# Pooled q, k and v of the first batch made by TensorE from the local blocks' tiles

## Chip, cores, metric

The kernel runs on one core of a Trainium2 chip. The metric is the time of one execution in device microseconds (us), the median of several runs. Engines: PE is TensorE's matmuls, PEld its weight loads, DVE VectorE, ACT ScalarE, POOL GpSimd, SP SyncE, which issues most DMAs; a q behind the name (SPq) is the engine's instruction queue.

## What is computed

An attention block feeds two mixtures of dense layers, all in float32. B, H, S, D = 4, 8, 576, 64.

```python
def _attn_ref(q, k, v):
    Sd = S // 4
    q_d = q.reshape(B, H, Sd, 4, D).mean(axis=3)   # k_d, v_d likewise
    ...
    out_d = sm_attn(q_d, k_d, v_d)                  # attention over 144 pooled tokens
    out_up = np.repeat(out_d, 4, axis=2)
    pos = np.arange(S)
    mask = np.abs(pos[:, None] - pos[None, :]) < 4  # local: 3 tokens to each side
    scores = scale * np.matmul(q, k.transpose(0, 1, 3, 2))
    scores = np.where(mask, scores, -1000000000.0)
    ...                                             # softmax
    out_local = np.matmul(attn, v)
    return out_up + out_local
...
x = attn_out.transpose(0, 2, 1, 3).reshape(2304, 512)
h = x @ w_in;  x = (h * np.cos(h)) @ w_out          # d_ff 2048
xn = x / rms * rms_g                                # second mixture, d_ff 1536
out = (silu(xn @ w_gate) * (xn @ w_val)) @ w_out2
```

## The kernel before

The program is written by generators, one for each piece of work. A planner (class Order) runs them against assumed costs and emits every engine's instructions in the order of its own clock, preferring early due times among what is ready; on the chip each engine then executes its list in order. Buffers and PSUM banks are tokens in pools (take, give); events tie generators together (wait, done). Where the planner sees TensorE idle in the first stretch, keep_warm (L251) emits filler matmuls of ident.

**First batch, pooled branch.** start() loads q and k of batch 0 in groups of four tokens, three column groups each (tile pq, L861). pq_first sums four tokens (sum4: q by one VectorE reduction, L385; k by two GpSimd additions, L380 and L382), transposes the sums on TensorE (trq, L425) and pq_ev copies them to PQ (pqs, L401). v comes in four head pairs of four loads each (values0, pv_load, L480 and L483; tile v4); pv sums them on GpSimd (L504 to L511) into vh, a block-diagonal tile. pooled() makes the scores (sps, L539), the softmax (L544 to L560), transposes the weights (tra, L575), multiplies by v (avp, L594) and copies the result to od (L602).

**Local blocks.** Each batch has five blocks of 116 queries (112 in the last) with 128 keys around them. block() takes one block's q and k (tile raw, loaded by raw_dma, L798, a token in each partition, 256 bytes to a descriptor), transposes them (btr, L646), multiplies them in 64x64 pieces (bs, L690), takes the softmax (L699 to L712), transposes the weights (bat, L726), waits for od, multiplies by v (bav, L752; v lies in one of three buffers vb, loaded by block_v, L814), adds od (L762) and rounds the sum into a high and a low part of x (L775 on ScalarE, L777 on GpSimd).

**First mixture.** Token tile 0 (256 tokens) needs the blocks 0, 1 and 2 of batch 0, tile 1 the blocks 2, 3 and 4. unit() computes h = x @ w_in for two chunks (h, L1013), second() the product with w_out (y, L1079). The weights are loaded as int32 words (L291, L293) and converted by w_conv on ScalarE, VectorE and GpSimd (L316 to L327). Two units of tile 0 come first, then tiles 0 and 1 take turns.

**Order of the loads.** SP issues them in program order: pq of batch 0, the mask bf, and then by a written list, where "w" is weight pieces, "r" a block's raw tiles, "v" all of v4:

```python
LOADS = (("w", 4), ("r", 1), ("v", 0), ("r", 1), ("w", 4), ("r", 3))
```

The early tiles lie in places that weights use later; 21 of the 31 places are held at first.

Of the kernel before, what the change touches and what calls it, by code (L numbers as in the profile page):

```python
# [9 lines left out]
F32 = mybir.dt.float32  # L10
# [3 lines left out]
ALU = mybir.AluOpType  # L14
# [23 lines left out]
LOADS = (("w", 4), ("r", 1), ("v", 0), ("r", 1), ("w", 4), ("r", 3))  # L38
# [17 lines left out]
class Order:  # L56
# [136 lines left out]
def fused_kernel(ctx: ExitStack, tc, q, k, v, w_in, w_out, w_gate, w_val, w_out2, rms_g, mask, bmask, out):  # L193
# [86 lines left out]
    def w_loads(m, pieces, src):  # L280

        for i in pieces:
            S_.due(conv_due(m, i) - 5.0)
            r = yield take("raw")
            p = yield take(PLACES, 1)
# [90 lines left out]
    def sum4(b, w, t, o, n):  # L376

        if b or w:
            yield "POOL", 0.05 + n * 0.32
            POOL.tensor_tensor(out=t[:, :n, 0:2], in0=t[:, :n, 0:2], in1=t[:, :n, 2:4], op=ALU.add)  # L380
            yield "POOL", 0.05 + n * 0.18
            POOL.tensor_tensor(out=o, in0=t[:, :n, 0], in1=t[:, :n, 1], op=ALU.add)  # L382
        else:
            yield "DVE", 0.05 + n * 0.27
            DVE.tensor_reduce(out=o, in_=t[:, :n].rearrange("p u r d -> p u d r"), axis=AX.X, op=ALU.add)  # L385
# [28 lines left out]
    def pq_first(w, c, t, qs, place):  # L414

        u0, n = UC[c]
        yield wait(("pq", w, c))
        yield from sum4(0, w, t, qs[:, u0:u0 + n], n)
        give("pqp", place)
        yield take("att")  # L420
        i = yield take("bank")
        ps = bank_tile(i, [64, 4, 128], "trq")
        yield "PE", 0.2 * n
        for x in range(n):
            PE.transpose(ps[:, x, :], qs[:, u0 + x, :], ident)  # L425
        yield from pq_ev(0, w, c, ps)
        give("bank", i)
        give("att", "att")
        count(("pq", 0), 6)
# [57 lines left out]
    def pv(b, hp, t=None, place=None, vh=None):  # L487

        vi = 0
        if b == 0:  # L490
            yield wait(("pv", hp))
        else:
            vi = yield take("vh")
            vh = VH[vi]
            p = []
            for _ in range(2):
                x = yield take("pq")
                p.append(x)
            t = (ap.tile([128, 512], F32, tag=p[0], name="v4").rearrange("p (c x) -> p c x", c=2),
                 ap.tile([128, 512], F32, tag=p[1], name="v4")[:, :256])  # L500
            yield from pv_load(b, hp, *t)
# [10 lines left out]
        if b == 0:  # L512
            give(place[2], place)
        else:
            for x in p:
                give("pq", x)
# [3 lines left out]
    def pooled(b, hp, E=None):  # L520
# [72 lines left out]
        for c in range(3):  # L593
            PE.matmul(o, vh[:, c], A[:, c], start=c == 0, stop=c == 2)  # L594
# [35 lines left out]
    def block(b, u, raw, pools):  # L630
# [9 lines left out]
        for w in range(2):  # L640
# [4 lines left out]
            for a in range(4):  # L645
                PE.transpose(t[:, a, :], raw[w][:, 2 * a:2 * a + 2].rearrange("t h d -> t (h d)"), ident)  # L646
# [107 lines left out]
        give("vb", v_i)  # L754
# [46 lines left out]

    def block_v():

        for b in range(B):
            for u in range(5):
                S_.due(blk_due(b, u) - 5.0)
                x = yield take("vb")
                VI[b, u] = x
                r0 = geo(u)[2]
                vp = v[b].rearrange("(a e) t d -> e t a d", e=2)  # L810
                for s, (_, _, kc) in enumerate(groups(u)):
                    for e in range(2):
                        yield "SP", 0.5
                        SP.dma_start(VB[x][64 * e:64 * e + 64, s], vp[e, r0 + kc:r0 + kc + 64])  # L814
                done(("rv", b, u))
# [26 lines left out]
    def start():  # L842
# [3 lines left out]
        for n in [("pq", w, c) for c in range(3) for w in range(2)] + [("qs", w) for w in range(2)] + [("E", hp) for hp in (1, 2, 3)] \  # L846
                + [("v4", hp) for hp in range(4)] + [("vhl", 0)] + [("raw", u) for u in range(5)]:
            pl[n] = yield take(PLACES)
# [4 lines left out]
        def load(ev, us):  # L853
            yield "SP", us

        qs = [early(("qs", w), [128, 9, 64]) for w in range(2)]
        for c, (u0, n) in enumerate(UC):
            for w in range(2):
                t = early(("pq", w, c), [128, 4, 4, 64])
                yield "SP", max(0.48, 0.37 * n)  # L860
                SP.dma_start(t[:, :n], pq_src(0, w, u0, n))  # L861
                done(("pq", w, c))
                S_.add(pq_first(w, c, t, qs[w], pl["pq", w, c]), 0.0, S_.now())
# [5 lines left out]
        for hp in range(4):  # L869
            S_.add(pooled(0, hp, E[hp]), 0.0)  # L870
        vh0 = early(("vhl", 0), [128, 2, 3, 128])
        vh0 = VH + [vh0[:, 0], vh0[:, 1]]
        for x in vh0:
            yield "POOL", 0.5
            POOL.memset(x, 0.0)
# [13 lines left out]
        def values0():  # L889
            for hp in range(4):  # L890
                t = early(("v4", hp), [128, 768])
                t = t[:, :512].rearrange("p (c x) -> p c x", c=2), t[:, 512:]
                yield from pv_load(0, hp, *t)
                done(("pv", hp))
                S_.add(pv(0, hp, t, pl["v4", hp], vh0[hp]), 0.0, S_.now())
# [7 lines left out]
        def raws(us):  # L903
            for u in us:
                t = early(("raw", u), [128, 2, 8, 64])
                for w in range(2):
                    yield from raw_dma(t[:, w], (q, k)[w], 0, u)
                done(("raw", 0, u))
                S_.add(block(0, u, (t[:, 0], t[:, 1]), (None, (pl["raw", u][2], pl["raw", u]))), blk_due(0, u))

        first = 0
        for what, n in LOADS:
            if what == "r":
                yield from raws(range(first, first + n))
                first += n
            elif what == "w":
                yield from words(n)
            else:
                yield from values0()
# [6 lines left out]
        S_.add(after("vhl", None, pl["vhl", 0]), 0.0)  # L926
        S_.add(after(("pq", 0), None, pl["qs", 0], pl["qs", 1]), 0.0)
# [5 lines left out]
        yield wait(("E2", 2))  # L933
        for _ in range(3):
            p = yield take("pqp")
            give(p[2], p)
# [911 lines left out]
```

## Time and profile before

| what | us |
|---|---|
| median of 3 runs (lowest to highest) | 983.76 (983.52 to 984.35) |
| profiled execution | 984.96 |
| its span in the profile | 983.1 |
| PE busy | 953.0 (97%) |
| PEld busy | 880.4 (90%) |
| DVE busy | 721.2 (73%) |
| ACT busy | 542.3 (55%) |
| POOL busy | 269.1 (27%) |

The span is the time from the first to the last recorded instruction; start times count from its beginning. Busy shares are means over stages with different limits. Ends of matmuls are modelled, so the length of a group of them is rough, while starts are not. A releaser behind an instruction is what ended the idle time before it.

### The profile page before, as it was taken

The numbers are of one execution on the slowest core, as the hardware profiler recorded it, in microseconds if no ns is written. First come the engines' busy times: TensorE is split into PE (matmuls) and PEld (weight loads), VectorE is DVE, ScalarE is ACT, GpSimd is POOL, SyncE is SP. The second block draws the span as 40 slices with busy tenths as digits, with TensorE's granted clock in tenths as the row PEclk, the third lists the DMA queues.
The fourth block names the chain that finished last, engine by engine and source line by source line (L and its number), as shares of the span: only waits on it lengthen the run. The fifth ranks groups of instructions, "written<-read, shape, count | busy, mean of one in ns | idle before, by whom it ended". The sixth has DMA issues, their size and how long they took to land.

```text
span 983.1 us, 19205 instructions
## 1 busy us (share of the span) xinstructions
PE 953.0 (97%) x7150; PEld 880.4 (90%) x7150; DVE 721.2 (73%) x1460; ACT 542.3 (55%) x1090; POOL 269.1 (27%) x325
## 2 busy tenths in 40 slices
PE   6789899999999999999999999999999999999998
PEld 6688778888988888888888889999999999999998
DVE  2789976677657775666577699586666688999895
ACT  3658886677677965656566465242322334554442
POOL 3877685544336311101042242000000014300000
PEclk9999999999999999999999999999999999999999
DMA  8788643567685554544331311133222144454432
GB/s 241 212 211 246 181 147 111 148 199 180 199 231 166 170 171 128 176 144 169 120 129 65 107 44 49 49 106 93 75 82 71 57 145 132 132 174 139 141 119 76
DMA packets 160333, 136.07 MB, mean 138 GB/s; under 512 B 72176, under 2 KB 133744, under 8 KB 160240
## 3 DMA queue, kind: packets, MB, share of 16 engines
q1 hardware_dynamic: 160240, 134.85, 45.8%
q8 instruction: 56, 0.92, 0.4%
q14 instruction: 37, 0.30, 0.1%
HBM read 98.64 MB, written 36.18 MB: 137 GB/s over the span
## 4 chain that ended last, share of the span: by engine, by line
PE 84%; DMA 4%; DVE 3%; SPq 3%; issue 2%; POOL 2%; ACT 2%; DVEq 0%; POOLq 0%; ACTq 0%
PE gvp L1502 26%; PE y L1079 19%; PE h L1013 18%; PE o L1755 13%; PE bav L752 2%; PE btr L646 1%; DMA pq<-in_q 1%; DMA raw<-in_k 1%; PE avp L594 1%; PE bs L690 1%; PE yt L1407 1%; POOL wwa L327 1%; PE bat L726 1%; PE sps L539 1%; DMA cst<-in_moe_rms_g 1%
## 5 line engine op out<-in xcount | busy, mean ns | idle before, releaser
L1502 PE MATMUL gvp<-xc,wc 128*128 128x384 f32 x1296 | 231.7, 335 | 0.0
L1502 PEld LDWEIGHTS gvp<-xc,wc 128*128 128x128 f32 x1296 | 225.6, 188 | 0.3
L1573 DVE TENSOR_TENSOR tmp<-gvp,tmp 128x384 f32<-128x384 f32 x180 | 99.3, 553 | 54.3 <-PE gvp L1502 51.0
L1013 PE MATMUL h<-big,wwa 128*128 128x256 f32 (+1 forms) x756 | 124.0, 316 | 0.9 <-DVE t L1038 0.5
L1755 PE MATMUL o<-wo,wc 128*128 128x256 f32 x972 | 118.4, 279 | 0.0
L1013 PEld LDWEIGHTS h<-big,wwa 128*128 128x128 f32 x756 | 107.5, 190 | 10.7 <-DVE t L1038 0.6
L1755 PEld LDWEIGHTS o<-wo,wc 128*128 128x128 f32 x972 | 115.7, 190 | 0.0
L1079 PE MATMUL y<-wwa,big 128*128 128x512 f32 x432 | 109.5, 397 | 0.7 <-DVE big L1049 0.7
L1079 PEld LDWEIGHTS y<-wwa,big 128*128 128x128 f32 x432 | 78.9, 188 | 17.7 <-DVE big L1049 1.6
L1013 PE MATMUL h<-big,wwb 128*128 128x256 f32 (+1 forms) x504 | 83.9, 317 | 0.4 <-DVE t L1038 0.3
L1079 PE MATMUL y<-wwb,big 128*128 128x512 f32 x324 | 82.0, 398 | 1.1 <-POOL big L1049 1.1
L1033 DVE SCALAR_TENSOR_TENSOR t<-kk,h 128x512 f32<-128x512 int32 x72 | 49.0, 681 | 44.1 <-ACT kk L1031 43.9
L1013 PEld LDWEIGHTS h<-big,wwb 128*128 128x128 f32 x504 | 72.0, 190 | 7.8 <-DVE t L1038 0.8
L1031 ACT ACTIVATE kk<-h 128x512 int32<-128x512 f32 x72 | 42.6, 592 | 58.1 <-PE h L1013 55.8
L1079 PEld LDWEIGHTS y<-wwb,big 128*128 128x128 f32 x324 | 59.0, 188 | 13.3 <-POOL big L1049 1.4
L1639 POOL TENSOR_TENSOR wt<-wo 128x256 f32<-128x256 f32 x10 | 9.8, 985 | 208.6 <-DVE wc L1358 183.4
L1038 DVE TENSOR_TENSOR t<-h,t 128x512 f32<-128x512 f32 x72 | 49.3, 686 | 17.9 <-ACT t L1036 17.4
L1564 ACT ACTIVATE tmp<-gvp 128x384 f32<-128x384 f32 x36 | 17.7, 492 | 75.8 <-PE gvp L1502 75.8
L1036 ACT ACTIVATE t<-t,cst 128x512 f32<-128x512 f32 x72 | 51.9, 722 | 13.4 <-DVE t L1033 12.9
L1047 ACT ACTIVATE big<-t 128x512 fp32r<-128x512 f32 x72 | 45.1, 628 | 25.1 <-DVE t L1038 23.7
L1698 ACT ACTIVATE wc<-ut 128x512 fp32r<-128x512 f32 (+1 forms) x60 | 34.3, 584 | 42.2 <-DVE ut L1684 25.3
L1049 DVE TENSOR_TENSOR big<-t,big 128x512 fp32r<-128x512 f32 x54 | 39.8, 738 | 16.6 <-ACT big L1047 16.3
(189 smaller groups left out, 1741.2 us busy)
## 6 DMA issues: line engine op xcount, KB each, us to landing
us<-tmp SPq DMA_DIRECT2D x72, 192.0 KB, 2.0
uf<-us SPq DMA_DIRECT2D x48, 256.0 KB, 3.0
rawwa<-in_moe_w_out SPq DMA_DIRECT2D x21, 512.0 KB, 4.3
wfs<-rawwa SPq DMA_DIRECT2D x36, 256.0 KB, 2.4
rawwa<-in_moe_w_gate SPq DMA_DIRECT2D x12, 512.0 KB, 4.3
rawwa<-in_moe_w_val SPq DMA_DIRECT2D x12, 512.0 KB, 4.6
wf<-wfs SPq DMA_DIRECT2D x12, 512.0 KB, 4.1
vb<-in_v SPq DMA_DIRECT2D x80, 64.0 KB, 2.8
```

The source lines that it names most:

```text
L1013: PE.matmul(h[:, w_ * ci:w_ * ci + w_], a[:, ksl], x_at(x, kk), start=m == 0, stop=m == 11)
L1031: ACT.activation(out=kk, in_=h, func=ACTF.Copy, scale=INV2PI, bias=0.25)
L1033: DVE.scalar_tensor_tensor(out=t, in0=kk, scalar=TWOPI, in1=h, op0=ALU.mult, op1=ALU.subtract)
L1036: ACT.activation(out=t, in_=t, func=ACTF.Sin, scale=-1.0, bias=cst[:, 0:1])
L1038: DVE.tensor_tensor(out=t, in0=h, in1=t, op=ALU.mult)
L1047: ACT.activation(out=gh, in_=t, func=ACTF.Copy)
L1049: (POOL if e == "POOL" else DVE).tensor_tensor(out=gl, in0=t, in1=gh, op=ALU.subtract)
L1079: PE.matmul(y[j][b], g[:, tsl], a, start=(first and ci == 0 and i == 0), stop=(last and c == 15 and i == 2))
L1502: PE.matmul(bank, w[:, a, kk], xc[:, x, b, kk], start=first and i == 0, stop=i == 5, skip_group_check=True)
L1573: DVE.tensor_tensor(out=half(o), in0=a, in1=half(b), op=ALU.add)
L1698: ACT.activation(out=o[:, 0], in_=src, func=ACTF.Copy)
L1755: PE.matmul(b[m][1][:, l], u[0][x][:, j, l], w[:, y, k], start=(p == 0 and l == 0 and i == 0), stop=(p == C3 - 1 and i == 2), skip_group_c ...
```

## The change

The pooled q and k of batch 0 are no longer loaded and summed by themselves. The blocks' q and k tiles now hold two neighbouring tokens in a partition: the 128 tokens of even heads are in partitions 0 to 63, those of odd heads in 64 to 127, with 512 bytes to a descriptor. q is loaded by SP and k by ScalarE (raw_half). For every block sums() multiplies these tiles by 0/1 matrices (M["q"], made by select() from ident), adding groups of four tokens and transposing in one step, and copies the result to PQ. vsums() does the same for v from the blocks' vb tiles, over all five blocks into two PSUM banks, and copies to vs. The block's transposes become matmuls with quarters of ident that put the tokens back in order. The product with pooled v uses two 64-row matmuls for each of three chunks where one 128-row matmul stood. Batch 0 has five v buffers instead of three, and its tiles load without waiting for one. The mask is loaded first, and the list of loads is written anew. 14 places are held at first. The batches 1 to 3 stay as they were, but for sum4, which sums q on GpSimd in them as before.

```diff
-LOADS = (("w", 4), ("r", 1), ("v", 0), ("r", 1), ("w", 4), ("r", 3))
+LOADS = (("r", 1), ("w", 1), ("r", 1), ("w", 1), ("r", 3), ("v", 1), ("w", 1), ("v", 1), ("w", 1), ("v", 1), ("w", 1), ("v", 1), ("w", 1), ("v", 1), ("w", 4))
...
-    def pq_first(w, c, t, qs, place):
...
+    def sums(u, raw):
+
+        _, n, _, off = geo(u)
+        m, j = n // 4, {0: 0, 3: 1, 16: 4}[off]
+        yield wait(("raw", 0, u))
+        yield wait("sel")
+        for w in range(2):
...
+            ps = bank_tile(i, [128, 4, 29], "pq")
+            yield "PE", 0.9
+            for a in range(4):
+                for r in range(2):
+                    for e in range(2):
+                        pr = slice(64 * e, 64 * e + 64)
+                        PE.matmul(ps[pr, a, :m], raw[w][pr, a, r], M["q"][pr, r if off == 3 else 0, 32 * e + j:32 * e + j + m],
+                                  start=a == r == 0, stop=a == 3 and r == 1, skip_group_check=True)
...
+                ACT.activation(out=o, in_=ps[:, :, :m], func=ACTF.Copy, scale=f)
...
+                DVE.tensor_scalar(out=o, in0=ps[:, :, :m], scalar1=f, scalar2=None, op0=ALU.mult)
...
+            count(("pq", 0), 10)
...
+    def vsums(vs):
...
+        for u in range(5):
+            yield wait(("rv", 0, u))
+            yield "PE", 1.6
+            for s in range(2):
+                f, t0, n, p0, p1 = VW[2 * u + s]
...
+                for c in sorted({p0 // 48, (p1 - 1) // 48}):
+                    x = 47 - (p0 - 48 * c)
+                    for e in range(2):
+                        pr = slice(64 * e, 64 * e + n)
+                        o = ps[c // 2][1][64 * e:64 * e + 64, c % 2]
+                        PE.matmul(o, M["v"][pr, f, x:x + 64], VB[VI[0, u]][pr, s],
+                                  start=(c // 2, e) not in seen, stop=False, skip_group_check=True)
...
+    def select(t):
...
+        POOL.memset(t[:, 0:512], 0.0)
...
+        DVE.tensor_reduce(out=q0, in_=ident[:, :].rearrange("p (x r) -> p x r", r=2), axis=AX.X, op=ALU.add)
...
         for c in range(3):
-            PE.matmul(o, vh[:, c], A[:, c], start=c == 0, stop=c == 2)
+            if b:
+                PE.matmul(o, vh[:, c], A[:, c], start=c == 0, stop=c == 2)
+                continue
+            for e in range(2):
+                pr = slice(64 * e, 64 * e + 64)
+                PE.matmul(o[pr], vh[pr, c, hp], A[pr, c], start=c == 0, stop=c == 2)
...
             for a in range(4):
-                PE.transpose(t[:, a, :], raw[w][:, 2 * a:2 * a + 2].rearrange("t h d -> t (h d)"), ident)
+                if b:
+                    PE.transpose(t[:, a, :], raw[w][:, 2 * a:2 * a + 2].rearrange("t h d -> t (h d)"), ident)
+                    continue
+                o = t[:, a].rearrange("p (x r) -> p r x", r=2)
+                for r in range(2):
+                    for e in range(2):
+                        pr = slice(64 * e, 64 * e + 64)
+                        PE.matmul(o[pr, r], raw[w][pr, a, r], ident[pr, pr], start=a == r == 0, stop=a == 3 and r == 1, skip_group_check=True)
...
+        def raw_half(eng, t, src, u, us):
+            for e in range(2):
+                yield "SP" if eng is SP else "ACT", us
+                eng.dma_start(t[64 * e:64 * e + 64], flat(src, (e * S + geo(u)[2]) * 64, [[128, 64], [2 * S * 64, 4], [1, 128]]))
+
+        def raws(us):
+            for u in us:
+                t = early(("raw", u), [128, 2, 4, 2, 64])
+                o = t.rearrange("p w a r d -> p w a (r d)")
+                S_.add(raw_half(ACT, o[:, 1], k, u, 0.3), 0.0, 0.0)
+                yield from raw_half(SP, o[:, 0], q, u, 0.9)
+                done(("raw", 0, u))
+                S_.add(sums(u, (t[:, 0], t[:, 1])), -40, S_.now())
+                S_.add(block(0, u, (t[:, 0], t[:, 1]), (None, (pl["raw", u][2], pl["raw", u]))), blk_due(0, u), S_.now())
...
-            S_.add(pooled(0, hp, E[hp]), 0.0)
+            S_.add(pooled(0, hp, E[hp]), -20)
...
+        vbx = early("vb", [128, 2, 2, 4, 64])
+        VB.extend(vbx[:, x] for x in range(2))
+
+        def values0(us):
+            for u in us:
+                x = NV + u - 3
+                if u < 3:
+                    x = yield take("vb")
+                yield from load_v(0, u, x)
+                if u == 0:
+                    S_.add(vsums(early("vs", [128, 3, 4, 64])), -20, S_.now())
```

## Rows read from the trace of the kernel before

**Rows 1.** Busy time by stretch: length, each engine's busy us (instructions), TensorE clock, DMA, GB/s.

```profile
0.00:18.00 18.00, 11.33 (x81) 10.73 (x82) 4.39 (x3) 4.10 (x8) 4.45 (x11) 1.00 0.76 207
18.00:70.00 52.00, 41.29 (x558) 37.64 (x556) 37.41 (x82) 32.54 (x92) 40.59 (x55) 1.00 0.83 230
70.00:140.00 70.00, 63.58 (x551) 55.90 (x549) 64.36 (x109) 57.84 (x111) 50.00 (x53) 1.00 0.68 196
140.00:165.00 25.00, 24.73 (x189) 21.71 (x190) 18.24 (x35) 19.23 (x41) 17.31 (x22) 1.00 0.42 131
165.00:983.00 818.00, 812.05 (x5778) 754.45 (x5777) 596.75 (x1232) 428.62 (x841) 156.80 (x187) 1.00 0.42 126
```

**Rows 2.** Groups by line and form, TensorE, 0 to 70 us: busy, mean ns.

```profile
L251 PE MATMUL warm<-ident 128*128 128x128 f32 x216 | 30.5, 289 | 1.4 <-POOL cst L233 1.4
```

**Rows 3.** Timeline, block 2's product to the first h: start us, length, engine, instruction.

```profile
66.44 1.14 PE L752 MATMUL bav<-bt,vb 64*64 64x58 f32 x32
...
69.38 0.59 POOL L777 TENSOR_TENSOR big<-bt,big 128x96 fp32r<-128x96 f32 x1 [0.28 <-ACT big L775]
...
69.87 1.73 PE L1013 MATMUL h<-big,wwa 128*128 128x256 f32 x12
```

**Rows 4.** Timeline, the pooled attention of batch 0.

```profile
21.69 2.48 PE L539 MATMUL sps<-pqs 64*72 64x144 f32 x32 [0.37 <-ACT pqs L401]
...
31.12 0.82 DVE L560 TENSOR_TENSOR E<-E,stat 72x288 f32<-72x288 f32 x2
...
46.81 1.04 PE L594 MATMUL avp<-at,vhl 128*128 128x144 f32 x6 [1.45 <-POOL vhl L510]
...
47.90 0.29 ACT L602 ACTIVATE od<-avp 128x144 f32<-128x144 f32 x1 [2.01 <-PE avp L594]
```

**Rows 5.** Busy time by stretch, instructions on the v4 tiles alone (GpSimd).

```profile
0.00:70.00 70.00, 15.51 (x24) 1.00 0.81 224
```

**Rows 6.** Tile raw, 0 to 70 us: issue ns min/median/max, first and last start.

```profile
L798 SPq DMA_DIRECT2D raw<-in_k x5: 434/581/1862, 17.5 to 55.1; - x5
```

**Rows 7.** Waits of SP's queue, 0 to 70 us: total, times, longest.

```profile
SPq L814 <- PE bav L752: 5.4, 2, 4.2
```

**Rows 8.** Timeline, load issues on SP.

```profile
1.18 2.70 SPq L814 DMA_DIRECT2D vb<-in_v  x4
...
38.22 3.60 SPq L436 DMA_DIRECT2D pq<-in_q  x1
```

**Rows 9.** Groups by line and form, VectorE, 0 to 70 us.

```profile
L322 DVE SCALAR_TENSOR_TENSOR rawwb<-rawwb 128x512 int32<-128x512 int32 x8 | 6.5, 808 | 0.2 <-ACT rawwb L320 0.2
L316 DVE TENSOR_SCALAR rawwb<-rawwb 128x512 int32<-128x512 int32 x9 | 4.8, 545 | 0.0
...
L385 DVE TENSOR_REDUCE qs<-pq 128x256 f32<-128x1024 f32 x2 | 3.8, 1886 | 11.8 <-DMA pq<-in_q 11.8
...
L712 DVE TENSOR_TENSOR bE<-bE,bst 128x512 f32<-128x512 f32 x3 | 3.2, 1062 | 0.1
...
L385 DVE TENSOR_REDUCE qs<-pq 128x64 f32<-128x256 f32 x1 | 0.6, 616 | 1.0 <-DMA pq<-in_q 1.0
```

**Rows 10.** Timeline, small matmuls of block 0.

```profile
26.03 0.63 PE L646 MATMUL btr<-ident,raw 128*128 128x128 f32 x4 [1.87 <-DMA raw<-in_q]
...
30.05 0.69 PE L690 MATMUL bs<-bt 64*64 64x64 f32 x32 [0.41 <-ACT bt L655]
```

**Rows 11.** Loads, 0 to 45 us: packets and rate; one kind's KB and us to landing.

```profile
DMA packets 14163, 10.56 MB, mean 235 GB/s; under 512 B 9070, under 2 KB 13038, under 8 KB 14160
...
vb<-in_v SPq DMA_DIRECT2D x12, 64.0 KB, 5.0
```

**Rows 12.** Timeline, one operation of VectorE beside GpSimd and later.

```profile
37.01 1.29 POOL L327 TENSOR_TENSOR wwa<-rawwb,wwa 128x512 fp32r<-128x512 f32 x1
37.23 1.62 DVE L712 TENSOR_TENSOR bE<-bE,bst 128x512 f32<-128x512 f32 x1
...
53.75 0.69 DVE L712 TENSOR_TENSOR bE<-bE,bst 128x512 f32<-128x512 f32 x1
```

More of the change, by code (lines that the diff above doesn't have):

```diff
@@ L284, in w_loads @@
             r = yield take("raw")
-            p = yield take(PLACES, 1)
+            p = yield take(PLACES if i < NF + NB - 1 else "wa", 1)
             raw = p[0].tile([128, 1024], I32, tag=p[1], name="raw" + p[1])
@@ L412, in count @@
             done(ev, XT[ev])
-    def pq_first(w, c, t, qs, place):
[L416 to L429, printed above, removed]
+    M = {}
@@ L485, in pv_load, with pv @@
                 SP.dma_start(tb[64 * e + n:64 * e + 64], flat(v, f0 * 64, [[256, 64 - n], [1, 256]]))
[L487 to L501, printed above, removed]
+    def pv(b, hp):
+        vi = yield take("vh")
+        vh = VH[vi]
+        p = []
+        for _ in range(2):
+            x = yield take("pq")
+            p.append(x)
+        t = (ap.tile([128, 512], F32, tag=p[0], name="v4").rearrange("p (c x) -> p c x", c=2),
+             ap.tile([128, 512], F32, tag=p[1], name="v4")[:, :256])
+        yield from pv_load(b, hp, *t)
         ta, tb = t[0].rearrange("p c (r d) -> p c r d", r=4), t[1].rearrange("p (r d) -> p r d", r=4)
@@ L511, in pv @@
             POOL.tensor_tensor(out=vh[pr, 2, 64 * e:64 * e + 64], in0=tb[pr, 0], in1=tb[pr, 1], op=ALU.add)
[L512 to L516, printed above, removed]
+        for x in p:
+            give("pq", x)
         vd[b, hp] = (vh, vi)
@@ L753, in block @@
         give("b2", a_i)
-        give("vb", v_i)
+        if v_i < NV:
+            give("vb", v_i)
+        else:
+            count("vb0", 2)
         t0 = (S_.cur["t"], "PE")
@@ L800, in fused_kernel, with load_v @@
     VI = {}
+    def load_v(b, u, x):
+        VI[b, u] = x
+        r0 = geo(u)[2]
+        vp = v[b].rearrange("(a e) t d -> e t a d", e=2)
+        for s, (_, _, kc) in enumerate(groups(u)):
+            for e in range(2):
+                yield "SP", 0.5
+                SP.dma_start(VB[x][64 * e:64 * e + 64, s], vp[e, r0 + kc:r0 + kc + 64])
+        done(("rv", b, u))
     def block_v():
-        for b in range(B):
+        yield wait(("rv", 0, 4))
+        for b in range(1, B):
             for u in range(5):
@@ L807, in block_v @@
                 x = yield take("vb")
[L808 to L815, printed above, removed]
+                yield from load_v(b, u, x)
     def blk_due(b, u):
@@ L845, in start @@
         pq_tiles(0)
[L846 to L847 removed]
+        for n in [("raw", u) for u in range(5)] + ["sel", "vb", "vs"] + [("E", hp) for hp in (1, 2, 3)] + [("E2", x) for x in range(3)]:
             pl[n] = yield take(PLACES)
@@ L851, in early @@
             return pl[n][0].tile(shape, dtype, tag=pl[n][1], name="".join(map(str, n)))
[L853 to L863, printed above, removed]
+        def raw_half(eng, t, src, u, us):
+            for e in range(2):
+                yield "SP" if eng is SP else "ACT", us
[9 more added lines that the diff above has]
+                S_.add(block(0, u, (t[:, 0], t[:, 1]), (None, (pl["raw", u][2], pl["raw", u]))), blk_due(0, u), S_.now())
+        S_.add(select(early("sel", [128, 512])), 0.0)
+        for x in range(3):
+            give("pqp", pl["E2", x])
         E = EP + [early(("E", hp), [72, 2, 3, 2, 64]) for hp in (1, 2, 3)]
@@ L901, in words @@
             yield from w_loads(1, range(i, nw[0]), w1_src)
[L903 to L911, printed above, removed]
+        first = {"r": 0, "v": 0}
         for what, n in LOADS:
[L913 to L916, printed above, removed]
+            if what == "w":
                 yield from words(n)
-            else:
-                yield from values0()
+                continue
+            i = first[what]
+            first[what] += n
+            yield from (raws if what == "r" else values0)(range(i, i + n))
         yield "SP", 0.96
```

80 lines of the change are left out of this document (56 added, 24 removed).

## The prediction

> **What bounds the kernel now.** I read the busy time by stretch first [rows 1]. From 165 us to the end TensorE is busy 812 of 818 us, so work that begins earlier there ends earlier by as much. Up to 70 us TensorE is busy too, but 30 of those 70 us are the filler matmuls of keep_warm [rows 2]; they keep the granted clock at 1.00 (2.4 GHz) and compute nothing. So the start is not bound by TensorE. Its product is the first matmul of the first mixture, h, at 69.87 us [rows 3].
>
> What h waits for is read backwards in the timeline. It needs x of token tile 0, so the blocks 0, 1 and 2 of batch 0. Block 2's last matmuls (bav) start at 66.44; the copy, the rounding on GpSimd and h follow, 3.43 us in all [rows 3]. A block's bav needs od, the pooled attention of the batch. The four head pairs' scores (sps) are there from 21.69, the weights are normalised on VectorE by 31.94, and yet the last od is copied at 47.90 to 48.19: its value product (avp) waited for GpSimd's sums of v [rows 4]. These sums keep GpSimd busy 15.5 us [rows 5]. From od to h another 21.7 us pass. There the local blocks are late: their q and k loads are issued one at a time between 17.5 and 55.1 us [rows 6], behind everything else on SP's queue, which also stood 5.4 us for block products to free a v buffer [rows 7], and once took 3.60 us over one load [rows 8].
>
> From 70 to 140 us VectorE is busy 64.36 of 70 us, ScalarE 57.84 and TensorE 63.58 [rows 1]. Weights are being converted there, and three engines are near full. That stretch decides how much of an earlier start is kept.
>
> **Removed.** Six pq loads of batch 0 (2.36 MB) and twelve v4 loads (1.57 MB); 15.5 us of GpSimd's v sums [rows 5], its k sums, two of four memsets; VectorE's three reductions, 3.8 + 0.6 = 4.4 us [rows 9]; 18 transposes of pooled rows with their copies. Also gone: the wait of SP for v buffers in batch 0, as five buffers now stand where three did.
>
> **Added on TensorE.** Per block and tensor 16 matmuls for the sums and 16 in place of four transposes, so 320 in five blocks, and 24 for v with 256 columns. Nearest in shape are the 32 score matmuls of a block, 64x64 by 64 columns, 0.69 us or 0.0216 us each [rows 10]. 320 of them are 6.9 us; the 24 count four times each, 2.1 us. From above, each of the 320 could cost what one transpose of a block does, 0.63 / 4 = 0.16 us [rows 10]: 50 us. I take 9 us, since the shape is the same; the 30 us of filler cover it, and bare it would cost 9. At the upper bound some 20 us would stand uncovered.
>
> **Added elsewhere.** VectorE gets the 0/1 matrices: eight small reductions, each at most the 0.62 us of the smaller L385 [rows 9], so 0 to 5 us; I take 1.5, since most read far fewer elements. It idles 13.6 of the first 18 us [rows 1], which hides them; without that cover the first sums would start up to 5 us later. Of twelve new copies out of PSUM it gets about half, an estimate of 2.3 us at 0.3 to 0.4 each (od's copy out of PSUM takes 0.29 [rows 4]). ScalarE issues ten k loads itself, at most 0.68 us each by an SP issue [rows 8], 6.8 us in a stretch where it is busy 4.1 of 18 us [rows 1]. Uncovered they would hold up the softmax behind them.
>
> **When the inputs land.** The blocks' q and k are 2.62 MB, two weight pieces stand among them, 1.05 MB; with the mask 3.74 MB at the 235 GB/s of the first 45 us [rows 11] take 15.9 us, so they land at about 18. The v of all five blocks (1.31 MB) and four more pieces (2.10 MB) follow: 7.15 MB or 30.4 us, landing at 31.5. By SP's issues: 32 of 0.675 us [rows 8] and six weights of about 0.5 make 24.6, and the landing time of vb is 5.0 [rows 11], so 30. I take 31.
>
> The Trainium skill speaks against hoping for more from ScalarE's queue: "DMA: Bandwidth & Descriptors", section "Issuing engines are not separate DMA queues", says that loads from several queues share the same 16 engines and only issue time is saved. No row here has ScalarE loading; by this rule the sum stands, and with doubled bandwidth the tiles would land about 8 us sooner.
>
> **When od is ready.** Sums and scores of the fifth block end about where they end now (18 plus some 2 us against 21.69), and the softmax takes the same 10.25 us (21.69 to 31.94) [rows 4]: 30 to 32. Values: 31 plus an estimate of 2 for the last matmuls and two copies, 33. Then four head pairs, each transposing, copying, multiplying, copying; the last step takes 1.4 us (46.81 to 48.19) [rows 4], and I allow 6 us for the four together: od at 39, 9 us sooner.
>
> **When h starts.** All raw tiles are there from 18 us, so VectorE sets the blocks' pace. It worked 37.4 us from 18 to 70 [rows 1]. Not needed before block 2's bav are four of the eight weight pieces (11.3 / 8 = 1.4 us each [rows 9], so 5.6) and the front halves of the blocks 3 and 4 (an estimate of 5). Added are 2.3, and some 3 us move ahead of 18 us. That leaves 26.1 us; at the 92% at which VectorE runs from 70 to 140 [rows 1] this is 28.4 us, so bav of block 2 at 46.4, and h 3.4 later, at 49.8. That is 20.0 us sooner than 69.87.
>
> **What is given back.** Before 69.87 TensorE has already done transposes and scores of the blocks 3 and 4, by the rows four times 0.63 and twice 0.69 plus masks [rows 10], about 5 us; part of it will still fit ahead of h, so I subtract 3.5 (bounds 1 and 5.5). Then the crowded stretch. VectorE's whole work to 165 us is 4.39 + 37.41 + 64.36 + 18.24 = 124.4 [rows 1]. With 4.4 less and 3.8 more it is 123.8. If 5 us are done by 18 and the rest goes at 92%, the same point is reached at 147, so 18 us sooner at most. The engine must hold that share for 129 us rather than 70 though, with fewer weight pieces ready when h starts; I subtract 4.5 us of new stalls of TensorE (bounds 0 and 14, the last if h stands as VectorE's backlog at 85% makes it: 18 + 118.8 / 0.85 = 158, a gain of 7, less what TensorE repeats).
>
> Sum: 20.0 - 3.5 - 4.5 = 12.0 us. The profiled execution took 984.96 us, its span 983.1, so 1.9 lie outside the span; span after 971.1, execution 973.0. The median of the three runs is 983.76, 1.2 under the profiled one: **972 us**.
>
> **Rivals.** A difference under 0.2% (2 us) can't be told from none.
>
> *All but the forecast is kept (chance 0.10, at 955 to 962).* VectorE gains more than counted. One normalisation of 128x512 (L712) took 1.62 us beside GpSimd's subtraction and 0.69 a little later [rows 12]; its three in the first 70 us average 1.06 [rows 9]. With 15.5 us of GpSimd's work gone, four such stretches save 3 to 4 us, h starts near 45, and 24 us less 1 to 3 are kept: 961. Against it: the backlog from 70 to 140. The Trainium skill has the rule in "SBUF — State Buffer", section "Who interferes with whom": a VectorE instruction with two SBUF inputs and a GpSimd one that reads SBUF block each other in full. The trace agrees (1.62 against 0.69 us).
>
> *The crowded stretch eats it (0.19, at 976 to 985).* VectorE's work hardly shrinks, and if weights come at their present pace, units wait for them whatever h's start was. With h 12 us sooner (late head pairs) and 5.5 + 5 given back, 1.5 us remain: 982. For it: 64.36 of 70 us. Against it: VectorE idles 28 of the first 70 us [rows 1], and a good part of that becomes usable. The matmuls at their upper price would end here too.
>
> *Slower (0.13, at 986 to 995).* All five v tiles, the last of them after 37 other loads on SP, now stand ahead of any od. If the queue stalls as at 38.22 [rows 8], v lands late, and od, all bav and h with it. Four head pairs and three bav with their tail take about 16 us from v's landing (31 to 39, three products of 1.14 us, 3.4, and waits). Equality needs h at 69.87 - 8 = 62, so v at about 46; each us beyond costs one. At 52 it is 990. For it: 20 issues of 3.6 us would be 72 us. Against it: the median landing of these tiles is 5.0 us, and fewer bytes are queued than now.
>
> **How the numbers follow.** The forecast (965 to 976) has 0.58, and the others 0.10, 0.19 and 0.13. Of the 0.19 about 0.07 lies within 2 us of now and 0.12 is faster. Faster is 0.58 + 0.10 + 0.12 = 0.80, same 0.07, slower 0.13. The range 960 to 984 leaves out the slower case and the fastest end.
>
> **What would show it.** Right: first h near 50, last od near 39, no SP wait on bav before it, filler of TensorE well under 30 us, VectorE over 90% from 20 us on, and a loss of TensorE of some 5 us more before its steady stretch, which then is as before. Wrong: v landing after 40; ScalarE idle behind its own loads; sums of over 2 us a block on TensorE; h at 50 but units waiting for weights until 160.

## The result, and the profile after

The changed kernel takes 990.79 us (median of six runs, 989.12 to 995.19), the kernel before 983.55 in the same session: ratio 1.0079, 95% interval 1.0059 to 1.0100. It is slower by 0.8%, and outside the predicted range of 960 to 984. The profiled execution took 989.12 us, span 986.8.

The first h starts at 73.88 us. [rows 3] have it at 69.87, so it is 4.0 us later, and the span is 3.7 us longer: the loss arises before h. Timeline of TensorE in the changed kernel, end of the start:

```profile
65.10 2.96 PE L828 MATMUL bav<-bt,vb 64*64 64x58 f32 x96
...
73.88 0.84 PE L1093 MATMUL h<-big,wwa 128*128 128x256 f32 x5
```

Busy time by stretch in the changed kernel, columns as in [rows 1]:

```profile
0.00:18.00 18.00, 12.79 (x154) 12.31 (x156) 2.07 (x9) 3.63 (x9) 4.63 (x14) 0.90 0.84 182
18.00:70.00 52.00, 51.04 (x941) 44.52 (x938) 32.85 (x78) 26.72 (x79) 14.61 (x13) 0.74 0.59 140
70.00:140.00 70.00, 62.11 (x582) 56.20 (x584) 65.39 (x100) 58.26 (x103) 54.63 (x53) 0.98 0.74 205
140.00:165.00 25.00, 24.65 (x181) 21.45 (x174) 20.70 (x39) 22.57 (x44) 14.16 (x17) 1.00 0.35 108
165.00:986.00 821.00, 812.74 (x5789) 754.04 (x5787) 601.43 (x1235) 431.73 (x862) 159.76 (x200) 1.00 0.42 127
...
13.00:14.00 1.00, 0.30 (x2) 0.19 (x2) 0.00 (x0) 0.27 (x1) 0.00 (x0) 1.00 1.20 200
...
15.00:16.00 1.00, 0.44 (x8) 0.44 (x10) 0.00 (x0) 0.00 (x0) 0.00 (x0) 0.50 1.09 186
...
18.00:30.00 12.00, 12.00 (x216) 11.37 (x214) 2.54 (x6) 4.56 (x10) 1.29 (x1) 0.50 1.09 209
30.00:44.00 14.00, 14.00 (x224) 12.60 (x223) 6.47 (x16) 3.19 (x7) 2.33 (x2) 0.50 0.85 222
...
46.00:50.00 4.00, 4.00 (x64) 2.97 (x63) 3.23 (x12) 1.91 (x9) 1.21 (x2) 1.00 0.43 136
```

The reader is to see two things in the second row. GpSimd has less to do from 18 to 70 us, as meant (14.61 against 40.59; over the whole span 247.8 against 269.1). VectorE has less there too (32.85 against 37.41), but that work only comes later: over the span it is busy 722.5 us against 721.2. And TensorE is now busy 51.04 of 52 us, at a granted clock of 0.74 in place of 1.00: from 14 to 45 us it runs at its lower level (0.50, 1.2 GHz). The start, which TensorE did not bound before, is bound by it up to 53.8 us. The page shows the fall in its row of forty slices:

```profile
PE   7999989999999999999999999999999999999998
...
PEclk7599999999999999999999999999999999999999
```

How it came to that is in TensorE's timeline (start, length, in brackets the idle time before):

```profile
8.92 1.12 PE L427 MATMUL pq<-sel,raw 64*64 64x29 f32 x32
9.87 1.13 PE L720 MATMUL btr<-ident,raw 64*64 64x64 f32 x32
...
13.64 0.30 PE L427 MATMUL pq<-sel,raw 64*64 64x29 f32 x2 [2.23 <-DMA raw<-in_k]
...
15.56 1.80 PE L427 MATMUL pq<-sel,raw 64*64 64x29 f32 x29 [1.62 <-DMA raw<-in_k]
...
19.89 1.91 PE L427 MATMUL pq<-sel,raw 64*64 64x29 f32 x32
...
28.45 1.96 PE L720 MATMUL btr<-ident,raw 64*64 64x64 f32 x32
```

A record is one line of the trace; x32 counts them. TensorE waited twice for k tiles, 3.85 us in all, with no filler matmul in between; the clock fell at the start of the second wait, and the same 32 records cost 1.9 us where they had cost 1.1. A wait of such a length alone does not bring it down: in the kernel before TensorE stood 2.46 us at 13.2 us, between runs of filler, and the clock stayed at 1.00 [rows 1]. How the k tiles came late is seen in ScalarE's timeline, and below it in two pieces of the chain that ended last (start, length from issue to landing):

```profile
6.76 6.80 ACTq L939 DMA_DIRECT2D raw<-in_k  x4
13.61 0.27 ACT L433 ACTIVATE pqs<-pq 128x116 f32<-128x116 f32 x1 [9.11 <-DMA raw<-in_k]
15.54 0.60 ACTq L939 DMA_DIRECT2D raw<-in_k  x1
...
21.85 3.48 ACTq L939 DMA_DIRECT2D raw<-in_k  x3
...
4.02 5.03 DMA raw<-in_q
9.06 6.45 DMA raw<-in_k
```

In this trace the loads of both queues use eight semaphores in turn, and an issue stands until the load that had its semaphore before has landed. The second k load of block 0 is issued at 9.06, when a q load of SP issued at 4.02 has landed. An issue itself takes 0.60 us (median); eight of the ten k issues begin within 0.03 us of the landing of an earlier load, and one (21.85) stands behind a copy that waits for TensorE. ScalarE's copies stand behind the issues in turn: the first sums of q were done at 10.04, and their copy starts at 13.61, when the fourth k load has been issued. So k shares the places with SP's loads of later blocks, of weights and of v. Block 0's k lands at 13.6 and 15.5, and the last k is issued at 23.8. Groups of TensorE from 0 to 70 us, busy time and mean, against [rows 2] and [rows 10]:

```profile
L427 PE MATMUL pq<-sel,raw 64*64 64x29 f32 x256 | 14.3, 276 | 3.8 <-DMA raw<-in_k 3.8
L720 PE MATMUL btr<-ident,raw 64*64 64x64 f32 x320 | 13.8, 247 | 0.0
L251 PE MATMUL warm<-ident 128*128 128x128 f32 x52 | 10.1, 368 | 1.4 <-POOL ident masks.py:199 1.4
L427 PE MATMUL pq<-sel,raw 64*64 64x28 f32 x64 | 3.8, 283 | 0.0
```

The sums (L427) and the new transposes (L720) are 160 matmuls each in the code, and 320 records each here: a matmul of this kind is recorded twice. Filler fell from 30.5 to 10.1 us. In the chain that ended last, every piece from 15.56 to 53.8 us is TensorE's: sums, transposes, score and v matmuls. Scores (sps) run at 42.3 and 48.7 where [rows 4] have the first at 21.69, and the last od is copied at 62.96 (47.90 there).

SP's queue, waits from 0 to 75 us (total, times, longest), against [rows 7]:

```profile
SPq L889 <- PE bav L828: 23.1, 1, 23.1
SPq L939 <- DMA raw<-in_q: 2.5, 2, 1.9
SPq L889 <- DMA raw<-in_q: 1.8, 2, 1.2
SPq L889 <- DMA rawwb<-in_moe_w_out: 1.5, 1, 1.5
SPq L293 <- DMA rawwa<-in_moe_w_in: 1.5, 1, 1.5
SPq L889 <- DMA vb<-in_v: 1.2, 1, 1.2
SPq L939 <- DMA rawwa<-in_moe_w_in: 0.9, 1, 0.9
```

The first row is SP standing from 43.0 to 66.1 us until a block product frees a v buffer; it holds back v and q of batch 1, which the first h does not read. The other six rows are issues that wait for earlier loads to land, 9.4 us in all.

### The profile page after: what moved, and what is told of

Its sections match the earlier page's. It is cut to its first block, busy times and chain, and to the rows that moved or that the text cites. A ratio compares the mean times of both kernels' runs of the same rounds, so it can differ in the third digit from the quotient of the medians.

```text
span 986.8 us, 20069 instructions
## 1 busy us (share of the span) xinstructions
PE 963.3 (98%) x7624; PEld 888.5 (90%) x7624; DVE 722.5 (73%) x1460; ACT 542.9 (55%) x1093; POOL 247.8 (25%) x296
## 4 chain that ended last, share of the span: by engine, by line
PE 84%; DVE 9%; DMA 3%; ACT 2%; issue 1%; SPq 0%; DVEq 0%; ACTq 0%
PE gvp L1582 26%; PE y L1159 17%; PE h L1093 17%; PE o L1835 13%; PE bav L828 2%; PE pq L427 2%; DVE rawwa L322 1%; PE sps L601 1%; PE bs L766 1%; PE btr L714 1%; PE btr L720 1%; DVE rawwb L322 1%; PE avp L657 1%; PE bat L802 1%; DMA raw<-in_k 1%
## 5 line engine op out<-in xcount | busy, mean ns | idle before, releaser
L1159 PEld LDWEIGHTS y<-wwb,big 128*128 128x128 f32 x324 | 58.8, 188 | 15.1 <-DVE big L1129 2.8
L1644 ACT ACTIVATE tmp<-gvp 128x384 f32<-128x384 f32 x36 | 17.7, 492 | 76.1 <-PE gvp L1582 76.1
L1129 DVE TENSOR_TENSOR big<-t,big 128x512 fp32r<-128x512 f32 x58 | 44.2, 762 | 13.2 <-ACT big L1127 12.8
```

The source lines that it names most:

```text
L1129: (POOL if e == "POOL" else DVE).tensor_tensor(out=gl, in0=t, in1=gh, op=ALU.subtract)
L1159: PE.matmul(y[j][b], g[:, tsl], a, start=(first and ci == 0 and i == 0), stop=(last and c == 15 and i == 2))
```

## The experiments

The first theory was: the small matmuls cost more than forecast, and still more at half clock, because removed filler left TensorE idle; so the q and k part loses and the v part gains. The rival theories were late k loads alone, and late v alone. Times are medians; each ratio is against the kernel before on the same chip; "lost" is the part of an earlier h that the span doesn't show, against 69.87 and 983.1 of before.

```
kernel                      us     ratio [95%]               first h   span    lost
changed kernel            990.79   1.0079 [1.0059, 1.0100]    73.9    986.8    -0.3
e1_fill                   987.87   1.0037 [1.0021, 1.0054]    71.6    989.6     4.8
e2_k_early                990.26   1.0056 [1.0038, 1.0075]    74.7    989.3     1.4
e3_half_sums              982.44   0.9964 [0.9944, 0.9984]    63.3    977.8     1.3
e4_v_only                 976.82   0.9912 [0.9884, 0.9940]    55.9    974.8     5.7
e5_fill2                  994.49   1.0107 [1.0086, 1.0128]    76.2    994.3     4.9
e9_qk_only               1003.23   1.0197 [1.0175, 1.0219]    74.2   1002.0    14.5
e10_v_only_scale          979.90   0.9958 [0.9940, 0.9977]    55.8    979.0     9.9
e11_k_on_sp               990.78   1.0070 [1.0055, 1.0085]    63.4    986.6    10.0
e12_fill3                 991.85   1.0087 [1.0072, 1.0102]    74.3    989.8     2.3
e14_v_only_early_g        975.98   0.9925 [0.9909, 0.9942]    55.0    974.1     5.8
e15_k_on_sp_half          986.38   1.0016 [0.9990, 1.0041]    65.0    987.7     9.5
e16_k_on_sp_t0            985.25   0.9995 [0.9972, 1.0018]    64.1    983.2     5.8
e17_v_only_t0             975.27   0.9908 [0.9890, 0.9925]    54.0    973.5     6.3
e18_v_only_t62            975.26   0.9914 [0.9890, 0.9939]    54.5    972.8     5.1
```

**e1_fill**: filler where TensorE first idles, in sums(u, w).

```diff
             i = yield take("bank")
+            if (u, w) == (0, 1):
+                f = bank_tile(i, [128, 128], "warm")
+                for _ in range(18):
+                    PE.matmul(f, ident, ident, start=True, stop=True, skip_group_check=True)
```

> The changed kernel with 18 filler matmuls of ident on TensorE ahead of the first block's k sums, where TensorE stood idle for 3.9 us (11.4 to 15.6 us) just before its clock fell to 0.50. Theory A, the idle stretch drops the clock and the half clock makes the start late: the granted clock from 18 to 50 us rises from 0.58 to 1.0, the sums take 1.1 us a group in place of 1.9, the first h comes 8 to 14 us sooner than 73.9, and the time is 977 to 983 us. Rival B, the many 64x64 matmuls bring the clock down by themselves: it still falls within the sums and the time stays at 988 to 993.

Measured 0.42% less than the changed kernel by the ratios, with h 2.3 us sooner. The clock stayed at 1.00 until 29 us and fell in the next idle stretch, which ended with a late k load (issued at 25.4) and ScalarE's copies behind it. TensorE's timeline in e1_fill:

```profile
24.99 2.05 PE L431 MATMUL pq<-sel,raw 64*64 64x29 f32 x64 [0.85 <-ACT pqs L437]
31.20 3.62 PE L431 MATMUL pq<-sel,raw 64*64 64x29 f32 x64 [4.16 <-ACT bt L735]
```

64 records took 2.05 us ahead of the gap and 3.62 behind it (clock 0.51 from 31 to 43). So idle time ahead of small matmuls goes with the fall, and the loads are next in line.

**e2_k_early**: all ten k loads issued by ScalarE ahead of its mask copies.

```diff
+        for u in range(5):
+            for _ in raw_half(ACT, rt[u].rearrange("p w a r d -> p w a (r d)")[:, 1], k, u, 0.3, True):
+                pass
         S_.add(select(early("sel", [128, 512])), 0.0)
```

> The changed kernel with ScalarE's ten k loads issued before its mask copies (from about 2.3 us in place of 6.8). Theory A: the k of block 0 lands as early as its q, the idle stretch of 3.9 us shrinks below 1, the clock stays at 1.0 and the time is 976 to 983 us, like the fillers or better. Rival B (the clock falls under the 64x64 matmuls): under 3 us of gain. Rival C (loads: both queues share the engines, so an earlier k only delays q): k earlier, q later, the gap moves, gain under 3 us.

No gain clear of the noise. The ten issues of 0.6 us are spread from 4.8 to 20.8 us, since each stands until an earlier load, first of all SP's, has landed. Block 0's k is complete at 15.1 us instead of 15.5; TensorE idled at 13 to 15 us and the clock was 0.50 from 15. Putting k first in ScalarE's list alone doesn't bring it sooner.

**e3_half_sums**: half of the sums' matmuls left out.

```diff
-                for r in range(2):
+                for r in range(1):
```

> The changed kernel with half of the sum matmuls of q and k left out (the second token of each partition is not added). Theory D, TensorE is what the start waits for from 16 to 54 us: 160 of 320 recorded matmuls go, at 58 ns each 9 us at the half clock, so the first h comes 7 to 9 us sooner and the time is 981 to 984. Rival C, loads set the pace (the last v lands at about 40 us): under 3 us of gain.

h 10.6 us sooner than in the changed kernel, the time 8.4 us less by the medians (1.15% by the ratios). The earlier h is more than the 160 records cost at half clock (5 times 1.9): the clock also came back sooner, as the windows show (length, TensorE's busy time; clock third from the end):

```profile
18.00:25.00 7.00, 7.00 (x122) 6.38 (x120) 2.54 (x6) 1.81 (x4) 0.00 (x0) 0.50 1.03 209
25.00:50.00 25.00, 23.82 (x486) 19.00 (x485) 21.45 (x54) 18.18 (x60) 11.21 (x10) 0.99 0.80 219
```

So TensorE's own work sets the start of the changed kernel.

**e4_v_only**: before, with only the v part: vsums, five v buffers, vs in place of vh; q and k loaded and summed as before.

```diff
-LOADS = (("w", 4), ("r", 1), ("v", 0), ("r", 1), ("w", 4), ("r", 3))
+LOADS = (("r", 1), ("w", 1), ("v", 1), ("r", 1), ("w", 1), ("v", 1), ("r", 1), ("w", 1), ("v", 3), ("w", 1), ("r", 2), ("w", 4))
```

> The kernel before with only the v part of the change: v pooled by TensorE from the blocks' v tiles, five v buffers, loads of v after the blocks' first tiles; q and k of the first batch are loaded and summed as before, the blocks' tiles keep a token a partition. If the v sums were the late part of the old start and the q and k part is what costs: pooled scores at 22 us as before, filler keeps the clock at 1.0, od at 38 to 43 in place of 48, first h at 57 to 63 in place of 69.9, time 973 to 979. If the crowded stretch after h eats every earlier start: h early but 982 to 985.

0.9912: faster than both kernels. TensorE's timeline in e4_v_only, last v matmuls and first h:

```profile
32.30 1.05 PE L455 MATMUL pv<-vb,sel 51*64 51x256 f32 x8
...
55.87 1.31 PE L1079 MATMUL h<-big,wwa 128*128 128x256 f32 x9
```

The last v matmul ends at 33.4, and h is 14.0 us sooner than before. TensorE's clock is 1.00 up to 50 us: 110 filler matmuls are left in the first 70 us and the long runs of small ones are missing.

**e5_fill2**: as e1, with fillers {(0,1): 18, (3,0): 4, (3,1): 20, (4,1): 8}.

> The changed kernel with filler in the second idle stretch as well (4, 20 and 8 filler matmuls ahead of the sums of the fourth block's q and k and the fifth block's k, on top of the 18), where the first fillers left TensorE idle from 27 to 31 us and its clock at 0.50 until 44. Theory A and C together (the first fillers won 11 us of TensorE's time, which the late k loads took back): granted clock 1.0 from 0 to 60 us, the stretch from 31 to 46 us shrinks by 5 to 7 us, first h at 64 to 68, time 979 to 984, and no lower, since k of the fourth block lands at 31 whatever the clock is. Rival B (64x64 matmuls bring the clock down): it falls in spite of the filler and the time stays at 987 to 990.

Slower than without. A wait of 2.1 us at 14.5 was still there, the clock fell near 19 and was back at about 32, against 45 in the changed kernel; the fillers themselves then stood on the path (h at 76.2).

**e9_qk_only**: the q and k part alone; v loaded and summed on GpSimd as before (vsums and its buffers taken out, v behind the five raw tiles and six weights behind v).

> The other half of the change alone: q and k of the first batch pooled by TensorE from the blocks' two-token tiles, k loaded by ScalarE, the mask first; v of the first batch is loaded by itself and summed on GpSimd as in the kernel before, with three v buffers. If q and k are what makes the change slower: pooled scores start at 36 to 44 us in place of 22, a clock of 0.5 to 0.8 from 18 to 50 us, and a time above the full change's or near it, 988 to 998. If instead v's place behind all other loads is what costs: the time is near that of before, 981 to 986.

1.0197, the slowest. h is about as late as in the changed kernel (74.2), but 14.5 us are lost behind it. GpSimd's longest wait before h:

```profile
POOL wwa L327 <- DMA v<-in_v: 27.2, 2, 24.8
```

The view names a v load, but the conversion at the end of the 24.8 us starts (30.74) ahead of the first v sum (35.69), just when ScalarE's part of it ends (30.66); ScalarE had stood 4.34 us in three k loads before that part. What the 14.5 us are made of isn't shown, so 2% is not the price of the q and k part alone. The parts don't add: +19.9 us for q and k alone, -7.4 for v alone, +7.2 together.

**e10_v_only_scale** and **e14_v_only_early_g**: e4 has VectorE wait 3.15 us at 42 us for the 2 KB of rms_g. e10 puts the scaling of them behind x(1); e14 only issues the load earlier, which is the edit shown.

```diff
             SP.dma_start(bf[64 * s:64 * s + 64], bmask[0:64])
+        SP.dma_start(gv_, rms_g.rearrange("(k p) -> p k", p=128))
...
-        SP.dma_start(gv_, rms_g.rearrange("(k p) -> p k", p=128))
```

> The v part alone, with the scaling of rms_g on VectorE set behind tile 1 of x, where it stood at 42 us and kept VectorE waiting 3.15 us for a load of 2 KB. If that wait is on the path to h: first h 2 to 3 us sooner than 55.9 and a time of 973 to 976. If the crowded stretch takes it: 976 to 978, as the v part alone. The planner orders what follows anew, which may hide a difference of this size.

> The v part alone, with the load of rms_g issued behind the mask's, and nothing else in the order of any engine changed, so that VectorE does not wait 3.15 us for it at 42 us. If that wait is on the path to h: first h at 53 to 55 in place of 55.9, time 974 to 976. If not: 976 to 978, as the v part alone.

e14 has h 0.8 us sooner and a time that can't be told from e4's. e10 is slower than either of its expectations: one small instruction was moved, and the planner wrote another order for everything behind it; h is as in e4, yet 9.9 us are lost.

**e11_k_on_sp**: k loaded by SP right behind q, block by block.

```diff
-                S_.add(raw_half(ACT, o[:, 1], k, u, 0.3), 0.0, 0.0)
-                yield from raw_half(SP, o[:, 0], q, u, 0.9)
+                yield from raw_half(SP, o[:, 0], q, u, 0.6)
+                yield from raw_half(SP, o[:, 1], k, u, 0.6)
```

> The changed kernel with the k tiles of the first batch loaded by SP, each right after its q, so that ScalarE issues no load. Theory C (ScalarE's queue holds the k loads of the blocks 2 to 4 behind copies that wait for TensorE: issued to 23.8 us, in the filled kernel to 29): all raw loads issued by 16 us, k of block 0 lands by 10, the idle stretch of TensorE before 16 us is under 2 us, the clock from 18 to 50 us is 0.8 or more, first h 6 to 10 us sooner than 73.9, time 980 to 985. Theory E, the transfers themselves are slow (512-byte pieces at about 190 GB/s with the engines full) and it matters little who issues them: the last k lands no sooner than 25 us, the clock falls as it did, and the time stays at 987 to 993.

The clock stays at 1.00 to 60 us, all raw tiles are issued by 17.7, and h starts at 63.4, 10.5 us sooner than in the changed kernel, though the same small matmuls run: they don't bring the clock down by themselves. By 17.7 us SP alone has issued 24 loads, as many as both engines in the changed kernel; but here all 20 q and k tiles are among them, there 15, with v and weights ahead of the rest. The time is the same. TensorE's timeline in e11_k_on_sp:

```profile
41.09 1.08 PE L465 MATMUL pv<-vb,sel 51*64 51x256 f32 x8
...
63.36 3.13 PE L1093 MATMUL h<-big,wwa 128*128 128x256 f32 x24
...
70.07 0.61 PE L251 MATMUL warm<-ident 128*128 128x128 f32 x4
74.50 0.66 PE L714 MATMUL btr<-ident,rqk 128*128 128x128 f32 x4 [3.83 <-DMA rqk<-in_q]
75.00 2.21 PE L251 MATMUL warm<-ident 128*128 128x128 f32 x10
```

At 70.7 TensorE comes to a transpose of batch 1 whose tile SP loaded late, having stood 10.2 us (its longest wait) for a bav to free a v buffer. Everything in its list waits behind. From 60 to 80 us TensorE is busy 15.04 of 20 (windows):

```profile
60.00:80.00 20.00, 15.04 (x158) 14.32 (x157) 13.64 (x21) 11.97 (x21) 12.38 (x13) 0.91 0.87 243
```

**e12_fill3**: as e1, with 28 fillers at (0,1) and 18 at (3,1).

> The changed kernel with 28 filler matmuls ahead of the first block's k sums and 18 ahead of the fourth block's, so that neither idle stretch seen with 18 fillers stays. Theory A and C: the clock stays at 1.0 from 0 to 60 us, the stretch up to the scores is ended by the loads and the doubled number of small matmuls, first h at 65 to 70, time 980 to 985: at the full clock the change is about level with the kernel before. Rival B, 64x64 matmuls bring the clock down by themselves: it falls between 18 and 28 us although no idle stretch over 1.2 us stands ahead of it, time 988 to 993.

The expectation failed: the clock was 1.00 to 30 us and fell in a wait from 29.3 to 32.8, which again ended behind ScalarE's k loads; it was back at 37. h is at 74.3, so the fillers cost what the clock gave. None of the three fillings mended the start with k on ScalarE.

**e15_k_on_sp_half** (e11 with e3's edit) and **e16_k_on_sp_t0** (e11 with the planner's T0, from which the due times of h, blocks and conversions are counted, at 60).

```diff
-T0, T1, U1, U2 = 70, 52, 6.5, 4.26
+T0, T1, U1, U2 = 60, 52, 6.5, 4.26
```

> The kernel of e11_k_on_sp with the matmuls that add the second token of each partition left out of the q and k sums, so part of the computation is missing: 160 of the 320 records of the sums, which at the full clock cost some 33 ns each (1.05 to 1.12 us per 32 records), 5 us in all. If TensorE's own time sets the start once the clock stays at 1.00, the first h comes about 5 us sooner than in e11, at 58 to 59 us. If the loads set it (v lands at about 41 us in e11), the first h stays at 62 to 64 us. The time is then 984 to 991 us, by how much of it the stretch after h gives back.

> The kernel of e11_k_on_sp with the planner's starting time set to 60 instead of 70 us, so that the order behind the first h is written for an h that starts where e11's does (63 us). If e11 lost its 10 us after h because the order was written for an h at 70 (tiles wait in order for loads that were given later due times), the time comes to 978 to 984 us with the first h again at 63 to 64. If the stretch itself (loads of the first expert beside the first chunks) is the limit, whatever the order, the time stays at 988 to 992 us.

e15: h at 65.0, not sooner than e11's 63.4, so with the clock at 1.00 the loads set the start and not the sums. Windows in e15_k_on_sp_half:

```profile
40.00:42.00 2.00, 0.96 (x4) 0.37 (x4) 1.97 (x6) 1.35 (x3) 1.53 (x3) 1.00 1.02 347
42.00:46.00 4.00, 3.88 (x46) 3.05 (x47) 3.35 (x8) 1.58 (x3) 2.16 (x2) 0.63 1.05 358
46.00:50.00 4.00, 4.00 (x34) 3.45 (x32) 3.00 (x9) 1.99 (x6) 0.14 (x1) 0.52 0.31 106
```

TensorE, with less to do, waits for the last v (40 to 42), and the clock falls behind that wait. Its median is below e11's, but its runs spread over 9 us and its profiled span is longer; that difference stays open.

e16: the same h (64.1), and 985.25 us, 5.5 under e11; the interval lies clear of e11's. It falls between the two expectations, nearer the first: what was lost behind h goes from 10.0 to 5.8 us. So some 4 us of e11's loss were the written order; what the rest is stays open. TensorE's wait at 70.7 is gone (busy 18.81 of 20 from 60 to 80).

**e17_v_only_t0** and **e18_v_only_t62**: e14 with T0 at 56 and at 62.

> The kernel of e14_v_only_early_g with the planner's starting time at 56 instead of 70 us, the time at which its first h starts (55.0). In e14 h came 14.9 us sooner than before and 5.9 us of that were lost behind it. If that loss comes from an order written for a later h, as e16's gain of some 5 us over e11 suggests, the first h stays at 55 to 57 and the time falls by 2 to 5 us, to 971 to 974. If the stretch behind h is limited by the engines themselves, whatever the order, the time stays at 975 to 978.

> As e17_v_only_t0, with 62 instead of 56 us, half way to the old value. By the order theory it lies between e14 and e17, at 973 to 976, with h at 55 to 57; by the theory that the engines limit the stretch it is 975 to 978, as e14.

Both can't be told from e14. In the v-only kernel the 5 to 6 us lost behind h don't come from T0. The fastest kernels of the study are these three and e4, 0.8 to 0.9% under before.

## Why the prediction was wrong

The forecast h was 49.8; the changed kernel's is 73.9, 24.1 us later. e11, in which the clock stays up, splits this: 10.5 us from 73.9 to its 63.4 (clock and late k together), 9.8 because the sums of v are copied by 42.8 there and not by 33, 3.1 for the four head pairs (od at 51.9, 9.1 us against 6), 0.7 from od to h (11.5 against 10.8).

**What bounds the kernel now** was read rightly of before, and the step from it to the changed kernel failed: from 15.6 to 53.8 us every piece of the chain is TensorE's.

**Removed** counts twelve v4 loads; there are sixteen, but their 1.57 MB are right.

**Added on TensorE**, with its cover, is the step that failed. It counted 320 matmuls rightly and priced them by the wrong row. The row of bs [rows 10] gives 0.0216 us a record, but each of those matmuls is two records, and they are spread over the four quadrants of the array. The sums and transposes use only the two quadrants of the diagonal, as bav does: its 32 records take 1.14 us [rows 3], 0.035 each. In these rows 0.035 holds for 29 to 64 columns, with accumulation and without; the quadrants fit the difference, though no run varies them alone. So 640 records at 0.035 make 22.4 us at full clock, in place of 6.9. v took 1.05 + 1.51 + 2.38 + 1.05 = 6.0 us in e4, in place of 2.1. Together 28.4 against the forecast 9 and the upper bound of 50. At full clock that price was not on the path: e15, with half of the sums left out of e11, has neither v's last matmul nor h any sooner. At the lower level it was: e3 brings h 10.6 us forward.

**The cover** failed with it. The 30 us of filler [rows 2] were taken as room for the new matmuls; the rows show that filler is also what stands in a wait for a load. The planner gives no filler from 11.4 to 15.6 us, the clock falls to 0.50, and up to 45 us TensorE's work takes some 1.7 times its time (1.91 against 1.12 us for 32 records). By an estimate from that, about 12 of those 30 us are the price; e11, where the clock stays up, has h 10.5 us sooner.

**Added elsewhere** was near for VectorE: its eight small reductions take 1.9 us against 1.5, and it makes two of the twelve copies. It weighed ScalarE's issues as a cost to ScalarE, and the first copy did stand 3.6 us behind them. What it left out is that these issues wait for earlier loads to land, so that k came late.

**When the inputs land.** The term for q and k, 18 us, was too small: they land by 21.3 in e11, with SP alone, and by 30.5 in the changed kernel. ScalarE's queue bought nothing. The Trainium skill has this in "DMA: Bandwidth & Descriptors", section "Issuing engines are not separate DMA queues": a second queue saves only the time of the issue. The traces agree (24 loads issued by 17.7 us with one queue and with two). v at 31 was 8 to 10 us early: it lands at 39.2 in the changed kernel and at 41.4 in e11, where this, and not TensorE, sets the start. The sum of issues (24.6) left out that SP itself waits for earlier loads to land: 9.4 us in the six rows above. 34.0 is then near the measured end of v's issues, 35.9. In e11 such waits are 0.9 us, but single issues of v last up to 2.0 us, and the last ends at 38.1. The mean rate up to 45 us was 206 GB/s, not 235.

**What is given back** was sized about right: 8.0 forecast, 5.1 to 6.3 in e4, e14, e17, e18 and e16. It doesn't hold throughout: e10, e11 and e15 lost some 10, e9 14.5.

**Rivals.** The outcome is on the side of *Slower*, by another mechanism: the last v load of the batch is issued at 35.3 and lands at 39.2, short of the 46 named there, while TensorE's matmuls held od up. *The crowded stretch eats it* named the matmuls' price, between forecast and upper bound, and didn't name the clock. That removing work from GpSimd and a serial load would pay was right for v: -7.4 us with the v part alone.

Open: what of the 10 us lost in e10, e11 and e15 is the order and what the crowded stretch; and what exactly brings the clock down and back.

## What to carry to other kernels

Price a small matmul by a row with the same shape and quadrants, in records and not in program matmuls. Before you count idle filler as free room, ask what TensorE does in each wait that stays; a wait with no filler can cost more than all that the change saves. A change in two parts is worth trying part by part: here one part alone gains 0.9% and the other alone loses 2%. When a load's issue moves to another engine, look at what the issue waits for, and at what stands behind it there.

## What was not expected of the hardware

The clock stayed at 0.50 from 15 to 44 us while TensorE was busy every microsecond (26 of 26 from 18 to 44, in rows above), mostly on 64x64 matmuls of 29 and 64 columns; it was back at 32 with some 128x128 filler among them (e5), and at 25 with half of the sums left out (e3). A second queue gave no more loads at a time, as this program has eight semaphores for both: an issue of 128 KB took 0.60 us on SP and on ScalarE alike (medians), but with both issuing, SP's last six of q were spread over 7.07 us and ScalarE's ten of k over 16 us (e2), each waiting for an earlier load to land. And the rate of small loads isn't told by packet size alone: from 5 to 15 us the changed kernel moved 239 GB/s in packets of 695 bytes in the mean (2.39 MB, 3438), e4 298 GB/s in packets of 524 (2.98 MB, 5684), most of them under 512 bytes (4540, against 191 of the changed kernel's).
